# Fewer products with ones: five operands a head, a starting product instead of zeros, one conversion step on ScalarE, and twelve weight slots

## The chip, the cores and the metric

One core of one Trainium2 chip runs the program once. The metric is the time of the program on the device in microseconds, the median of several runs. Engines are named as in the profile: PE is TensorE (PEld its weight loads), DVE is VectorE, ACT is ScalarE, POOL is GpSimd, SP is the engine that issues all transfers here.

## What is computed

Three stages follow each other, all in float32 as seen from outside.

```python
# attention over 4 x 8 heads, 1152 keys, 576 pooled queries, head size 64
q_pool = q.reshape(B, H, S // 2, 2, D).mean(axis=3)
scores = scale * np.matmul(q_pool, k.transpose(0, 1, 3, 2))
scores = scores - np.max(scores, axis=-1, keepdims=True)
attn = np.exp(scores)
attn = attn / (np.sum(attn, axis=-1, keepdims=True) + 1e-09)
x = np.matmul(attn, v)                       # then (2304, 512)
# soft mixture of 8 experts, 4 slots each
logits = x @ phi
d = softmax over tokens;  slot_input = d.T @ x
slot_out[e] = np.maximum(slot_input[e] @ w1[e], 0.0) @ w2[e]
x = (softmax over slots) @ slot_out
# a last feed-forward layer
h = x @ w_in
out = np.where(h >= 1, h, np.where(h <= -1, 0.0, (h + 1) ** 2 / 4)) @ w_out
```

The feed-forward weights w_in and w_out come in as float64 words and are converted to float32 on the chip, in 32 pieces, while attention runs.

## The kernel before, in words

**Attention.** Heads are worked on in 16 pairs. A pair has 9 steps c of 128 keys, and each step has two halves h = 0, 1, one for each head. In this text (c,h) is a half step. The order of every half step is written out by hand under `manual_schedule`, the loop at the end of the printed code: `max_half` (scores 11 steps ahead, of the next pair or the one after it, 4 products on PE and a maximum `mp` on DVE, L309 and L321), `st` (scores of the present pair, 8 products, L375, and the exponentials `e` on ACT, L380), `es_sum` in some half steps (L397), `pv` of the step before (the product with v, L410), and then what the table `sched` holds for this half step, put there by `plan` and by the list `CVS`. Three PSUM tiles go round under the names `mx` and `st`: a product for the maximum and a score product take the next one each, so `st` of a half step can start only when the `mp` of the half step before has read its tile.

**The row sums.** The sum over keys of the exponentials is a product with a column of ones, into columns behind the product with v in the two tiles `acc`. Which steps are first added up on DVE stands in `GRP`: before, steps 0 and 1, 2 and 3, 4 and 5 are added in pairs (`es_add`, L387, three additions a head), and 6, 7 and 8 go in as they are: six operands a head. `TAT` says in which half step which operands are multiplied: operand 0 in (3,1), 1 in (5,1), 2 and 3 in (7,1), 4 and 5 in (9,0), which is (0,0) of the next pair. Every operand takes 8 products, which the trace counts as 16 since a float32 product is two instructions. Before the first product with v, in (1,0) and (1,1), two products with a column of zeros (L407) write zeros to the used columns of each `acc` tile, and everything after them accumulates.

**The conversion.** Piece n of the feed-forward weights is loaded (`cv_load`, tile `f`, two buffers), converted on DVE in four steps (`cv_step` 0 to 3, tile `wst`, two buffers), and stored. Step 0 is two instructions, L191 (take off the sign) and L192 (clamp). For n below 16 ACT makes a rounded copy `whi` and DVE the rest (`cv_lo`, L215), a fifth step. `CVS` lists the eleven half steps of each pair in which one such step is put; the work starts in pair 0 and ends in pair 13. Piece n + 2 is loaded as soon as step 3 of piece n is over.

**The experts' weights.** 36 blocks of 1 MB (`w1`, `w2`, then four blocks `wi` of the converted w_in) are loaded in a fixed order into 23 slots of 8 KB a partition, which open as attention's pools close, and one more, `w_last`. The last 12 blocks go into slots that are used a second time: `w_load` takes slot (i - NSL - 1) % NWA, with NWA = 10, when `w_used` has told that the slot was read. So blocks wi 2 and wi 3 wait for the two first blocks of the second half of `w2`. All transfers are issued by SP in program order.

## Time and profile before

| | us |
|---|---|
| median of 3 runs | 807.64 (806.80 to 808.34) |
| the profiled execution, its own time | 807.59 |
| its span in the trace | 805.4 |
| PE busy | 781.2 (97%) |
| DVE busy | 558.8 (69%) |
| ACT busy | 434.0 (54%) |
| POOL busy | 130.4 (16%) |
| mean granted TensorE clock | 0.992 of full speed |

The times in the trace count from the span's start. Attention takes the stretch from about 33 to 530 us, the experts that up to about 590, the feed-forward layer the rest. PE is called busy while any product is in its pipe, so neighbouring products overlap in the rows; the step from one start to the next tells what a group costs PE. The same holds for DVE, where a row of 0.75 us is followed by the next start after 0.67.

### The profile page before, as it was taken

What the parts mean: (1) busy time and instruction counts of PE and PEld (TensorE: products, weight loads), DVE (VectorE), ACT (ScalarE), POOL (GpSimd) and SP (SyncE); (2) the same over time, 40 slices, a digit from 0 to 9 for tenths busy, and PEclk for the clock granted to TensorE, in tenths of its full rate; (3) what the DMA queues carried; (4) which work ended last, traced back from release to release, by engine and by line L of the source; (5) the groups of instructions that cost most, each with busy time, mean ns of one, the idle gap of its engine ahead of it and who ended that gap; (6) DMA issues with size and microseconds to landing.
All of it is one profiled execution on the core that took longest, in us unless ns stands there. A gap on an engine that the chain in (4) does not pass through costs nothing.

```text
span 805.4 us, 19576 instructions
## 1 busy us (share of the span) xinstructions
PE 781.2 (97%) x8216; PEld 562.7 (70%) x8216; DVE 558.8 (69%) x879; ACT 434.0 (54%) x823; POOL 130.4 (16%) x104
## 2 busy tenths in 40 slices
PE   7899999999999999999999999999999999999998
PEld 6676766666766766667665676663478888888887
DVE  6878888787898787878977864225286777666620
ACT  4346556565665565565555645621276777565620
POOL 7000000000000000000000000000244445434330
PEclk8899999999999999999999999999999999999999
DMA  9777758897988778787897761869980000000000
GB/s 212 179 161 174 206 153 204 230 229 184 239 220 215 207 181 215 211 204 217 195 223 213 189 190 16 313 229 375 393 312 26 27 27 1 26 27 27 27 26 27
DMA packets 144103, 135.51 MB, mean 168 GB/s; under 512 B 80912, under 2 KB 100624, under 8 KB 143632
## 3 DMA queue, kind: packets, MB, share of 16 engines
q1 hardware_dynamic: 144016, 134.28, 60.6%
q8 instruction: 64, 1.05, 0.5%
q14 instruction: 23, 0.19, 0.1%
HBM read 91.29 MB, written 17.30 MB: 135 GB/s over the span
## 4 chain that ended last, share of the span: by engine, by line
PE 80%; DVE 9%; ACT 4%; DMA 4%; issue 2%; SPq 1%; ACTq 0%; DVEq 0%
PE st L375 16%; PE acc L410 14%; PE po L1025 8%; PE po L1024 8%; PE po L1026 8%; PE mx L309 7%; PE acc L397 7%; DVE mp L321 4%; ACT e L380 3%; PE h L961 2%; PE tx L447 2%; PE h L777 2%; DMA q<-qn 1%; PE s2o L829 1%; PE tb L474 1%
## 5 line engine op out<-in xcount | busy, mean ns | idle before, releaser
L380 ACT ACTIVATE e<-st 128x576 f32<-128x576 f32 x288 | 187.3, 652 | 162.3 <-PE st L375 156.6
L321 DVE TENSOR_REDUCE mp<-mx 128x1 f32<-128x576 f32 x282 | 211.2, 751 | 78.7 <-PE mx L309 77.9
L410 PE MATMUL acc<-e,vf 128*64 128x288 f32 x1152 | 195.3, 412 | 0.6 <-ACT e L380 0.6
L309 PE MATMUL mx<-K,q 128*64 128x288 f16 x1152 | 124.4, 296 | 8.6 <-DVE mp L321 5.4
L375 PE MATMUL st<-q,K 128*64 128x288 f16 x1152 | 121.9, 288 | 6.0 <-DVE mp L321 2.5
L375 PE MATMUL st<-q,S 128*64 128x288 f16 x1152 | 121.9, 286 | 0.4 <-DMA q<-qn 0.4
L309 PEld LDWEIGHTS <-q 128*64 128x64 f16 x1152 | 64.7, 111 | 68.7 <-issue 22.2
L974 DVE TENSOR_TENSOR r<-cl,r 128x1024 f32<-128x1024 f32 x34 | 81.2, 2388 | 38.6 <-ACT cl L973 38.6
L1025 PE MATMUL po<-wlo,ghi 128*128 128x512 f32 (+1 forms) x280 | 107.6, 384 | 0.0
L1024 PE MATMUL po<-whi,ghi 128*128 128x512 f32 (+1 forms) x280 | 107.6, 384 | 0.0
L1026 PE MATMUL po<-whi,glo 128*128 128x512 f32 (+1 forms) x280 | 107.2, 383 | 0.0
L980 POOL TENSOR_TENSOR glo<-r,ghi 128x1024 fp32r<-128x1024 f32 x34 | 81.7, 2403 | 101.6 <-ACT ghi L979 99.3
L375 PEld LDWEIGHTS <-K 128*64 128x64 f16 x1152 | 68.1, 109 | 28.4 <-issue 19.2
L277 POOL TENSOR_TENSOR qf<-qf 128x576 f32<-128x576 f32 x14 | 20.8, 1483 | 402.9 <-DMA qf<-in_q_dram 282.4
L410 PEld LDWEIGHTS acc<-e,vf 128*64 128x64 f32 x1152 | 75.9, 136 | 13.2 <-ACT e L380 1.8
L387 DVE TENSOR_TENSOR es<-e,e 128x576 f32<-128x576 f32 x96 | 70.7, 739 | 7.8 <-PE acc L397 7.8
L375 PEld LDWEIGHTS <-S 128*64 128x64 f16 x1152 | 69.8, 110 | 3.3 <-issue 0.6
L964 ACT ACTIVATE r<-h,cols 128x512 f32<-128x512 f32 x68 | 42.8, 685 | 32.8 <-PE h L961 31.3
L1026 PEld LDWEIGHTS po<-whi,glo 128*128 128x128 f32 x280 | 52.6, 188 | 10.5
L1024 PEld LDWEIGHTS po<-whi,ghi 128*128 128x128 f32 x280 | 52.7, 188 | 9.7
L1025 PEld LDWEIGHTS po<-wlo,ghi 128*128 128x128 f32 x280 | 52.7, 188 | 9.2
L965 DVE TENSOR_SCALAR cl<-h 128x512 f32<-128x512 f32 x68 | 43.7, 686 | 18.2 <-ACT r L964 16.7
(192 smaller groups left out, 838.2 us busy)
## 6 DMA issues: line engine op xcount, KB each, us to landing
w<-in_moe_w_dram SPq DMA_DIRECT2D x31, 1024.0 KB, 8.2
vf<-in_v_dram SPq DMA_DIRECT2D x16, 576.0 KB, 4.9
kf<-in_k_dram SPq DMA_DIRECT2D x30, 288.0 KB, 3.6
f<-in_moe_w_out_dram SPq DMA_DIRECT2D x16, 512.0 KB, 4.9
f<-in_moe_w_in_dram SPq DMA_DIRECT2D x16, 512.0 KB, 5.9
qf<-in_q_dram SPq DMA_DIRECT2D x30, 256.0 KB, 4.4
S<-K SPq DMA_DIRECT2D x16, 288.0 KB, 6.3
out_dram<-ob SPq DMA_DIRECT2D x17, 256.0 KB, 2.0
```

The costliest lines, as they stand in the source:

```text
L309: nc.tensor.matmul(ps[p0:p1, i, 0:HQ], lhsT=q1[P][:, t, p0:p1], rhs=kk[:, j * HQ:(j + 1) * HQ], start=True, stop=True)
L321: nc.vector.tensor_reduce(out=mp[P][:, t, a:a + 1], in_=ps[:, :, 0:HQ], op=ALU.max, axis=AX.XY)
L375: nc.tensor.matmul(ps[c0:c0 + 64, i, 0:HQ], lhsT=kk[:, ci, c0:c0 + 64], rhs=f[:, sl[i]], start=first, stop=not first)
L380: nc.scalar.activation(out=e, in_=ps[:, :, 0:HQ], func=AF.Exp, scale=ESC)
L387: nc.vector.tensor_tensor(out=Es[P, n, h], in0=a, in1=b, op=ALU.add)
L397: nc.tensor.matmul(acc[P, i][32 * j:32 * j + 32, HQ:HQ + c1 - c0], lhsT=ones.to_broadcast([128, 32]), rhs=src[:, j % 2, c0:c1], start=Fals ...
L410: nc.tensor.matmul(acc[P, i][h * 64:(h + 1) * 64, 0:HQ], lhsT=vt[P][:, h, c, :], rhs=E[P, c, h][:, i, :], start=False, stop=(c == NK - 1))
L974: nc.vector.tensor_tensor(out=r[:, sl], in0=cl[:, sl], in1=r[:, sl], op=ALU.add)
L980: nc.gpsimd.tensor_tensor(out=glo[n, qd][:, sl], in0=r[:, sl], in1=ghi[n, qd][:, sl].bitcast(F32), op=ALU.subtract)
L1024: nc.tensor.matmul(po, lhsT=ghi[n, qd][:, j, sl], rhs=whi[:, f, cs], start=(f == 0), stop=False)
L1025: nc.tensor.matmul(po, lhsT=ghi[n, qd][:, j, sl], rhs=wlo[:, f, cs], start=False, stop=False)
L1026: nc.tensor.matmul(po, lhsT=glo[n, qd][:, j, sl], rhs=whi[:, f, cs], start=False, stop=(f == 15))
```

## The change

It does four things.

1. `GRP` now adds steps 0 to 4 up on DVE (four additions a head, eight a pair, in the half steps (2,h) to (5,h)) and leaves 5 to 8 alone: five operands a head. `TAT` multiplies operands 0, 1, 2 in (7,0) and 3, 4 in (9,0), and nowhere else.
2. The products with zeros are gone. The first product with v starts the accumulation itself (`start=(c == 0)`).
3. L191, the first instruction of conversion step 0, becomes an absolute value on ACT (`cv_abs`), issued for piece n + 1 right behind step 3 of piece n. `CVS` is another list of eleven half steps; (0,0) and (7,0) now hold two steps each.
4. The pool of two weight slots `w0` stays open as long as the first ten, and twelve slots go round instead of ten.

```diff
-CVS = (0, 1), (1, 0), (3, 1), (4, 0), (4, 1), (5, 0), (5, 1), (6, 0), (7, 0), (8, 0), (8, 1)
+CVS = (0, 0), (0, 0), (0, 1), (3, 1), (4, 1), (6, 0), (7, 0), (7, 0), (7, 1), (8, 0), (8, 1)
...
-GRP = ((0, 1), (2, 3), (4, 5), (6,), (7,), (8,))
-TAT = ((3, 1, (0,)), (5, 1, (1,)), (7, 1, (2, 3)), (9, 0, (4, 5)))
+GRP = ((0, 1, 2, 3, 4), (5,), (6,), (7,), (8,))
+TAT = ((7, 0, (0, 1, 2)), (9, 0, (3, 4)))
...
+    NWL = NWA + NW0
...
-            sl = i if i < NSL else (i - NSL - 1) % NWA
+            sl = i if i < NSL else (i - NSL - 1) % NWL
...
-            if (i if i < NWA else i - NWA + NSL + 1) not in gone:
+            if (i if i < NWL else i - NWL + NSL + 1) not in gone:
...
+    def cv_abs(n):
+        t, dst = cv[n][0], g2.tile([128, 512], F32, tag="wst", bufs=2, name=f"wst{n}")
+        cv[n] = t, dst
+        nc.scalar.activation(out=dst, in_=t[:, :, 1].bitcast(F32), func=AF.Abs)
+
     def cv_step(n, i):
...
-            nc.vector.tensor_scalar(out=d, in0=t[:, :, 1], scalar1=0x7fffffff, scalar2=None, op0=ALU.bitwise_and)
             nc.vector.tensor_scalar(out=dst, in0=dst, scalar1=CLO, scalar2=CHI, op0=ALU.max, op1=ALU.min)
...
             if n + 2 < 32:
                 cv_load(n + 2)
+            if n + 1 < 32:
+                cv_abs(n + 1)
...
     def pv(P, c, i):
         if c == 0:
             acc[P, i] = acc_tile(i, f"acc{P}_{i}")
-
-            n = HQ + (192 if i == 0 else HQ - 192)
-            z = ident.bitcast(F16)[:, 0:n // 2].unsqueeze(1).to_broadcast([128, 2, n // 2])
-            for h in range(2):
-                nc.tensor.matmul(acc[P, i][h * 64:(h + 1) * 64, 0:n].rearrange("p (a b) -> p a b", a=2),
-                                 lhsT=zcol.bitcast(F16)[:, 0:1].to_broadcast([128, 64]), rhs=z, start=True, stop=False)
         for h in range(2):
             nc.tensor.matmul(acc[P, i][h * 64:(h + 1) * 64, 0:HQ], lhsT=vt[P][:, h, c, :], rhs=E[P, c, h][:, i, :],
-                             start=False, stop=(c == NK - 1))
+                             start=(c == 0), stop=(c == NK - 1), skip_group_check=True)
...
+        at(CVS[CV0 - 1][0], 0, cv_abs, 0)
...
-                    pool = wtop.enter_context(tc.tile_pool(name=nm, bufs=1, side="right"))
+                    pool = (wx if nm == "w0" else wtop).enter_context(tc.tile_pool(name=nm, bufs=1, side="right"))
```

Three places show how instructions move. First PE in pair 6. Before, the products with ones stand in four places; this is the one in (3,1), between the scores and the product with v (`es6_0_0` is the sum of steps 0 and 1 of head 0, `x2` the two products that differ in the rows written):

```order
L397 MATMUL acc6_0_3457<-es6_0_0_3520,cols_71 32x192 x2
L397 MATMUL acc6_0_3457<-es6_0_1_3544,cols_71 32x192 x2
L397 MATMUL acc6_1_3485<-es6_0_0_3520,cols_71 32x96 x2
L397 MATMUL acc6_1_3485<-es6_0_1_3544,cols_71 32x96 x2
L410 MATMUL acc6_1_3485<-e6_2_0_3509,vf6_2981 64x288
L410 MATMUL acc6_1_3485<-e6_2_1_3540,vf6_2981 64x288
```

With the change nothing of them is left in (3,1), and (7,0) of the same pair has three operands in a row, the sum of steps 0 to 4 and steps 5 and 6 as they are:

```order
L401 MATMUL acc6_0_3377<-es6_0_0_3433,cols_71 32x192 x2
L401 MATMUL acc6_0_3377<-es6_0_1_3457,cols_71 32x192 x2
L401 MATMUL acc6_1_3400<-es6_0_0_3433,cols_71 32x96 x2
L401 MATMUL acc6_1_3400<-es6_0_1_3457,cols_71 32x96 x2
L401 MATMUL acc6_0_3377<-e6_5_0_3593,cols_71 32x192 x2
L401 MATMUL acc6_0_3377<-e6_5_1_3613,cols_71 32x192 x2
L401 MATMUL acc6_1_3400<-e6_5_0_3593,cols_71 32x96 x2
L401 MATMUL acc6_1_3400<-e6_5_1_3613,cols_71 32x96 x2
L401 MATMUL acc6_0_3377<-e6_6_0_3633,cols_71 32x192 x2
L401 MATMUL acc6_0_3377<-e6_6_1_3660,cols_71 32x192 x2
L401 MATMUL acc6_1_3400<-e6_6_0_3633,cols_71 32x96 x2
L401 MATMUL acc6_1_3400<-e6_6_1_3660,cols_71 32x96 x2
```

Four places have become two, and the other two operands stand in (0,0) of the next pair as two did before.

Second DVE in the same pair, from (3,0) to (5,0); each `mp` row opens a half step. Before, with conversion steps of piece 12 (`wst12`) in (3,1), (4,0), (4,1) and (5,0):

```order
L321 TENSOR_REDUCE mp7_3265<-mx7_5_0_3546 128x1
L287 SCALAR_TENSOR_TENSOR qn2_0_104<-qf8_3288,qn1_106 128x9x64
L321 TENSOR_REDUCE mp7_3265<-mx7_5_1_3574 128x1
L194 TENSOR_SCALAR wst12_3465<-wst12_3465 128x512
L321 TENSOR_REDUCE mp7_3265<-mx7_6_0_3612 128x1
L387 TENSOR_TENSOR es6_1_0_3635<-e6_2_0_3509,e6_3_0_3561 128x576
L197 SCALAR_TENSOR_TENSOR wst12_3465<-f64_12_3183,wst12_3465 128x512
L321 TENSOR_REDUCE mp7_3265<-mx7_6_1_3638 128x1
L387 TENSOR_TENSOR es6_1_1_3665<-e6_2_1_3540,e6_3_1_3589 128x576
L200 SCALAR_TENSOR_TENSOR wst12_3465<-f64_12_3183,wst12_3465 128x512
L321 TENSOR_REDUCE mp7_3265<-mx7_7_0_3672 128x1
L215 TENSOR_TENSOR wst12_3465<-wst12_3465,whi12_3668 128x512
```

And now:

```order
L325 TENSOR_REDUCE mp7_3169<-mx7_5_0_3459 128x1
L391 TENSOR_TENSOR es6_0_0_3433<-es6_0_0_3433,e6_2_0_3422 128x576
L291 SCALAR_TENSOR_TENSOR qn2_0_104<-qf8_3216,qn1_106 128x9x64
L325 TENSOR_REDUCE mp7_3169<-mx7_5_1_3488 128x1
L391 TENSOR_TENSOR es6_0_1_3457<-es6_0_1_3457,e6_2_1_3453 128x576
L199 SCALAR_TENSOR_TENSOR wst12_3289<-f64_12_3141,wst12_3289 128x512
L325 TENSOR_REDUCE mp7_3169<-mx7_6_0_3519 128x1
L391 TENSOR_TENSOR es6_0_0_3433<-es6_0_0_3433,e6_3_0_3474 128x576
L325 TENSOR_REDUCE mp7_3169<-mx7_6_1_3543 128x1
L391 TENSOR_TENSOR es6_0_1_3457<-es6_0_1_3457,e6_3_1_3503 128x576
L202 SCALAR_TENSOR_TENSOR wst12_3289<-f64_12_3141,wst12_3289 128x512
L325 TENSOR_REDUCE mp7_3169<-mx7_7_0_3578 128x1
```

Every half step from (2,0) to (5,1) now has one addition; conversion steps are left only in (3,1) and (4,1), and the others have gone to (6,0) and later.

Third SP in pair 8, around (6,1) and (7,0), where the transposing load of the next pair's second operand (`q2`) and the six loads of k and q for pair 11 are issued. Before, the store of piece 17 and the load of piece 19 stood ahead of them:

```order
L207 DMA wi_dr_76<-wst17_4654 128x512
L180 DMA f64_19_4746<-in_moe2_w_in_dram 128x1024
L358 DMA_TRANSPOSE q2_9_4786<-qn2_1_105 128x9x128
L233 DMA kf11_4828<-in_k_dram 128x576 x2
L241 DMA qf11_4831<-in_q_dram 128x4x128
L242 DMA qf11_4831<-in_q_dram 128x4x128
L243 DMA qf11_4831<-in_q_dram 64x128
L244 DMA qf11_4831<-in_q_dram 64x128
```

Now they stand behind:

```order
L362 DMA_TRANSPOSE q2_9_4647<-qn2_1_105 128x9x128
L237 DMA kf11_4711<-in_k_dram 128x576 x2
L245 DMA qf11_4714<-in_q_dram 128x4x128
L246 DMA qf11_4714<-in_q_dram 128x4x128
L247 DMA qf11_4714<-in_q_dram 64x128
L248 DMA qf11_4714<-in_q_dram 64x128
L209 DMA wi_dr_76<-wst17_4349 128x512
L181 DMA f64_19_4721<-in_moe2_w_in_dram 128x1024
```

The absolute value of piece 19, which needs both (the load, and the buffer that the store reads), stands on ACT in (8,1) of the same pair, behind the exponentials of that half step.

## Rows read from the trace of the kernel before

**Rows 1.** The profile page, chain of waits that ended last, shares by engine.
```profile
PE 80%; DVE 9%; ACT 4%; DMA 4%; issue 2%; SPq 1%; ACTq 0%; DVEq 0%
```

**Rows 2.** Busy us (instructions) by stretch: PE, PEld, DVE, ACT, POOL, clock, DMA share, GB/s.
```profile
221.52:252.41 30.89, 30.08 (x407) 21.29 (x403) 26.16 (x44) 18.52 (x42) 2.54 (x2) 1.00 0.82 211
477.23:504.96 27.73, 27.66 (x380) 19.39 (x376) 13.11 (x22) 15.67 (x35) 0.00 (x0) 1.00 0.22 41
```

**Rows 3.** Timeline of PE, pairs 5 and 6: start us, us, engine, line, what.
```profile
217.91 1.19 PE L397 MATMUL acc<-e,cols 128*32 128x192 f32 x32
219.03 0.71 PE L410 MATMUL acc<-e,vf 128*64 128x288 f32 x4
...
221.52 0.37 PE L407 MATMUL acc<-ident,cols 128*64 128x480 f16 x2
221.72 0.66 PE L410 MATMUL acc<-e,vf 128*64 128x288 f32 x4
...
222.94 0.33 PE L407 MATMUL acc<-ident,cols 128*64 128x384 f16 x2
223.10 0.66 PE L410 MATMUL acc<-e,vf 128*64 128x288 f32 x4
...
230.26 0.70 PE L397 MATMUL acc<-es,cols 128*32 128x192 f32 x16
230.88 0.71 PE L410 MATMUL acc<-e,vf 128*64 128x288 f32 x4
```

**Rows 4.** Timeline of PE, pair 6: products for the maximum at five half steps.
```profile
220.78 0.42 PE L309 MATMUL mx<-K,q 128*64 128x288 f16 x4
...
226.12 0.44 PE L309 MATMUL mx<-K,q 128*64 128x288 f16 x4 [0.57 <-DVE mp L321]
...
238.91 0.41 PE L309 MATMUL mx<-K,q 128*64 128x288 f16 x4
...
240.13 0.41 PE L309 MATMUL mx<-K,q 128*64 128x288 f16 x4
...
241.35 0.41 PE L309 MATMUL mx<-K,q 128*64 128x288 f16 x4
```

**Rows 5.** Timeline of DVE, pair 6, half steps (5,1) and (6,0).
```profile
238.39 0.42 DVE L191 TENSOR_SCALAR wst<-f 128x512 int32<-128x512 int32 x1
238.84 0.43 DVE L192 TENSOR_SCALAR wst<-wst 128x512 f32<-128x512 f32 x1
239.37 0.76 DVE L321 TENSOR_REDUCE mp<-mx 128x1 f32<-128x576 f32 x1
240.04 0.75 DVE L387 TENSOR_TENSOR es<-e,e 128x576 f32<-128x576 f32 x1
240.71 0.42 DVE L194 TENSOR_SCALAR wst<-wst 128x512 int32<-128x512 int32 x1
```

**Rows 6.** Groups of ACT by line: busy us, mean ns, then idle time before.
```profile
L204 ACT ACTIVATE whi<-wst 128x512 fp32r<-128x512 f32 x16 | 10.1, 631 | 6.7 <-DVE wst L200 4.7 <-DVE mm L354 1.8
```

**Rows 7.** Timeline of SP at the end of pair 6.
```profile
242.25 2.12 SPq L358 DMA_TRANSPOSE q<-qn  x1
...
247.79 0.53 SPq L180 DMA_DIRECT2D f<-in_moe_w_out_dram  x1
```

**Rows 8.** Tiles f (first) and wst (second): from issue to landing.
```profile
DMA to landing us min/median/max: 3.7/5.7/7.2
DMA to landing us min/median/max: 2.3/4.6/6.6
```

**Rows 9.** Timelines of POOL and DVE, end of pair 1.
```profile
92.22 1.42 POOL L277 TENSOR_TENSOR qf<-qf 128x576 f32<-128x576 f32 x1 [28.45 <-DMA qf<-in_q_dram]
92.71 1.22 DVE L191 TENSOR_SCALAR wst<-f 128x512 int32<-128x512 int32 x1
```

**Rows 10.** Busy us of a stretch among the experts (columns of rows 2), and the chain there.
```profile
562.00:566.00 4.00, 4.00 (x44) 1.16 (x36) 0.62 (x8) 0.00 (x0) 0.00 (x0) 1.00 1.05 387
574.71 8.08 DMA whi<-wo_dr
```

More of the change, by code (lines that the diff above doesn't have):

```diff
@@ L181, in cv_load @@
         cv[n] = t, None
+    def cv_abs(n):
+        t, dst = cv[n][0], g2.tile([128, 512], F32, tag="wst", bufs=2, name=f"wst{n}")
+        cv[n] = t, dst
+        nc.scalar.activation(out=dst, in_=t[:, :, 1].bitcast(F32), func=AF.Abs)
     def cv_step(n, i):
         t, dst = cv[n]
-        if dst is None:
-            dst = g2.tile([128, 512], F32, tag="wst", bufs=2, name=f"wst{n}")
-            cv[n] = t, dst
         d = dst.bitcast(I32)
         if i == 0:
-            nc.vector.tensor_scalar(out=d, in0=t[:, :, 1], scalar1=0x7fffffff, scalar2=None, op0=ALU.bitwise_and)
             nc.vector.tensor_scalar(out=dst, in0=dst, scalar1=CLO, scalar2=CHI, op0=ALU.max, op1=ALU.min)
@@ L397, in es_sum @@
                     nc.tensor.matmul(acc[P, i][32 * j:32 * j + 32, HQ:HQ + c1 - c0], lhsT=ones.to_broadcast([128, 32]),
-                                     rhs=src[:, j % 2, c0:c1], start=False, stop=False)
+                                     rhs=src[:, j % 2, c0:c1], start=False, stop=False, skip_group_check=True)
     def pv(P, c, i):
```

## The prediction

> **What bounds the kernel now.** I read the chain of waits first: PE holds 80% of it and DVE 9% [rows 1], so time is won where PE has less to do, and lost where DVE makes PE wait. Then I cut attention into pairs of heads. Pair 6 takes 30.89 us, with DVE busy for 26.16 of it; pair 14, which has no conversion and DVE busy for 13.11, takes 27.73 [rows 2]. The reader is to see two things in these rows: the clock is 1.00, the higher of its two levels (2.4 GHz), in both, so it explains nothing; and a pair with a loaded DVE is 3.2 us longer. About 1 us of that is products for maxima that pair 14 no longer has (those of its last four half steps, 0.3 each, estimated as 4 of the 16 products of a clean half step, which takes 1.22 us from 240.13 to 241.35 [rows 4]). Some 2 us a pair are therefore time in which PE waits for DVE. One such wait stands in the timeline, 0.57 us before the product at 226.12 [rows 4].
>
> **The products with ones.** In the timeline a place with two operands costs PE 1.12 us from its start to the next group's (217.91 to 219.03), a place with one 0.62 (230.26 to 230.88) [rows 3]. So a further operand in the same place costs 0.50. Before: two places with two and two with one, 2 x 1.12 + 2 x 0.62 = 3.48 us a pair. After: one with three (1.12 + 0.50 = 1.62) and one with two, 2.74. That is 0.74 a pair off PE.
>
> **The zeros.** Their two groups take 0.20 and 0.16 us from start to start [rows 3], 0.36 a pair. Nothing follows in their place: the first product with v now waits for its exponentials and for the emptied tile at once, and both were there before, since the zeros ran without a wait in these rows.
>
> Together PE has 1.10 us less in each of 16 pairs, 17.6 us. All of it lies on PE's own path, unless DVE now ends last. (In the last pair exponentials have four buffers, so those of (7,0) wait for the products with ones of the same half step, up to 1.62 us; PE needs them two half steps later, which covers it.)
>
> **VectorE's load.** An addition costs 0.67 from start to start (240.04 to 240.71), a maximum 0.67, the removed L191 0.45 (238.39 to 238.84) [rows 5]. Two additions a pair more are 32 x 0.67 = 21.4 us; 32 times L191 less are 14.4. So DVE gets 7 us more in all, some 0.5 a pair, and PE 1.1 less: the two come close, and the place decides. I cut the pair in two.
>
> From (1,0) to (5,1) a pair now takes 238.91 - 220.78 = 18.13 us [rows 4]. The zeros and both places with one operand (0.62 each) lie there, so 18.13 - 0.36 - 1.24 = 16.53 would be left with the same waits. DVE has to do there, after the change: ten maxima and eight additions (18 x 0.67 = 12.1), three splits of k and q of the same size (2.0), two conversion steps (1.0), and 0.3 of small work, 15.4 in all. That fits, with 1.1 to spare, and it is spread evenly, one addition a half step, where before conversion steps and additions met in (4,0), (4,1) and (6,0). The other eight half steps get PE 0.50 longer, 12.76 + 0.50 = 13.26, and DVE there has eight maxima, nine short conversion steps and little else, about 10.3. So I expect waits to shrink, not to grow. Bounds of this term: between nothing and the 1.1 to spare, in the 13 pairs with conversion; I take 0.5, nearer to the timeline's waits of half a microsecond than to the end, 6.5 us in all.
>
> **The absolute value on ScalarE.** No row shows this function. The nearest is the copy of the same size on ACT, 0.631 us [rows 6]; the lower bound is the 0.45 that DVE took. ACT is busy for 18.5 of 30.9 us in pair 6 [rows 2], so 32 x 0.63 = 20 us more hide there, and no queue but ACT's own exponentials stands behind them. The Trainium skill, ScalarE: Activation LUTs, Rules for kernel authors, speaks against this: elementwise work of that kind belongs on VectorE, which is faster. The rows agree on speed (0.45 against 0.63) but not on the price here: by the page the move loses 6 us of engine time, by the rows it takes 14 off the engine that PE waits for, and the sum is the same either way.
>
> What counts is what the absolute value waits for. It is issued early, one piece ahead, and needs the load of its piece and the store that empties its buffer. Where that load is issued in (7,0) or later, it stands on SP behind the transposing load of `q2` and six loads of k and q: SP starts the first at 242.25 and comes to the load of `f` at 247.79, 5.5 us on [rows 7]. With the usual 5.7 to the landing [rows 8] that is 11.2 us. In pairs 5, 8 and 12 the absolute value that needs it is in (8,1), which ACT reaches about 7 us after 242.25 (1.62 + four clean half steps of 1.22 and the exponential). So ACT would stand for some 4 us with the next exponentials behind it, and PE, which can go on for two half steps, would lose 2 to 2.5 each time: I take 7 us for the three. In seven more pieces the same load is needed one or two half steps later, and the products with ones of (0,0) cover it. Bounds: 0, if it lands early, and 23 if all ten cost 2.3.
>
> **Twelve slots.** The two last blocks of w_in no longer wait for the two first blocks of the second half of `w2`. But in that stretch the transfer engines are full, 1.05 of their time at 387 GB/s, and the chain there is the landing of `whi` [rows 10], which stands behind the same bytes as before. Issuing earlier only lengthens the queue: I take 0, and 1.5 either way as bounds.
>
> **The sum.** The profiled execution took 807.59, within 0.1 of the median. 807.6 - 17.6 - 6.5 + 7 = 790.5; I say 790.5.
>
> **The rivals.**
>
> *VectorE becomes the bound and it gets slower.* Eight additions in ten half steps make `mp` late, PE waits for the tile, and (1,0) to (5,1) stays at 18.1 us. Then a pair takes 18.13 + 13.26 = 31.39, 0.5 more than now: + 6.5 in 13 pairs, - 3.3 in the three without conversion, + 7 for the late absolute values, 818; 811 without those. It turns slower once the stretch is above 17.6. For it: DVE will be busy for some nine tenths of a pair. Against: 15.4 is well below 17.6. I give it 0.06. Half of it (a stretch of 17.3, pairs of 30.6) gives about 807, no change: 0.05.
>
> *ScalarE stands for every late load.* All ten cost 2.3: 790.5 + 16 = 806.5. Against: the later ones have 2 to 3 us more time. 0.05.
>
> *GpSimd in the way.* When its addition runs (92.22 to 93.64), L191 beside it takes 1.22 instead of 0.42 [rows 5, 9]. This addition comes about (0,1), and the change puts three conversion steps into (0,0) and (0,1). At 0.8 in each of 13 pairs, all on the path, that is 10.4 us: 801. PE has the products with ones in (0,0) to cover half: 796. 0.08. The Trainium skill, GPSIMD Engine Reference, Specifications, states the same as a rule: the two engines share their access to SBUF, and VectorE instructions that read two inputs from it contend too. By that rule the additions would be hit as well, but they lie in (2,0) to (5,1), and the trace shows GpSimd at work at the end of a pair only.
>
> *It all works.* No late landing, and the whole 1.1 comes back: 807.6 - 17.6 - 14.3 = 776. 0.10.
>
> **How the numbers follow.** My forecast has the remaining 0.66. The range runs from 780 (half of the best case's further gain) to 801 (GpSimd on the whole path, or the forecast with waits that do not shrink and one and a half times the late loads); what is left out is most of the slower and the unchanged cases and the lower half of the best, about 0.2. A run can be told from no change from 0.2% on, 1.6 us. Faster by more: 0.66 + 0.08 + 0.10 and a part of ScalarE's case, 0.86. Within: 0.05. Slower: 0.09, VectorE's case and the rest of ScalarE's.
>
> **What will show it.** Right: the products with ones on PE fall from 1536 to 1280 (six operands to five, 16 rows each, 16 pairs), and no product with zeros is left; the distance from one pair's (1,0) to the next is near 29.3 in an ordinary pair; DVE has no wait of an addition for `acc`; ACT's absolute values take about 0.63; ACT shows three or so waits for `f` or `wst` of some microseconds, at the ends of pairs 5, 8 and 12. Wrong on the DVE step: PE rows with waits for `mp` in (2,0) to (5,1), and a pair of 30.5 or more. Wrong on the ACT step: exponentials that wait behind absolute values in most pairs. Wrong on the slots: `whi` landing earlier after the last product of attention than now. What would make the whole prediction wrong is a DVE that, with nine tenths of its time taken, cannot keep its maxima in step.

## The result, and the profile after

The changed kernel takes 800.18 us (five runs, 796.57 to 803.1), the kernel before 807.9 beside it (five runs, 806.8 to 808.34): ratio 0.9906, 95% interval 0.9888 to 0.9925. It is 7.7 us faster where 17.1 were forecast; the time lies in the range, near its slow end. The profiled execution took 803.1, 2.9 above the median, with a span of 801.0.

The page's chain of waits, shares by engine, then by line, answers to [rows 1]:

```profile
PE 73%; DMA 10%; ACT 6%; DVE 6%; issue 3%; SPq 1%; ACTq 0%; DVEq 0%
PE st L379 14%; PE acc L408 13%; PE po L1024 8%; PE po L1023 8%; PE po L1025 8%; PE mx L313 7%; PE acc L401 4%; ACT e L384 3%; DMA f<-in_moe_w_in_dram 2%; DVE mp L325 2%; DMA wi<-wi_dr 2%; PE h L960 2%; DMA wo_dr<-wst 2%; PE h L776 2%; DMA wo_dr<-whi 2%
```

DVE has left part of the chain (9% to 6%), and DMA has come in (4% to 10%): the load of `f` and the stores of `whi` and `wst`, none of which this line names for the kernel before. (The load of `wi` comes behind attention, where the time did not change.)

Of the 4.4 us between the two profiled executions 3.5 lie in attention, from its first score product (`st`) to the start of the last, in (8,1) of pair 15. Behind that start nothing is won: 278.3 us to the end of the span before, 278.7 after (spans less 527.06 and 522.29). Another 1.3 lie ahead of the first score product, at 32.2 before and 30.9 after; over the runs below that start lies anywhere from 29.8 to 32.5, so nothing is read from it.

Busy time by stretch (columns of [rows 2]), after the change, for pair 6, pair 10 and pair 14, each from the first score product of (1,0) to the same in the next pair:

```profile
219.11:248.31 29.20, 28.87 (x384) 20.92 (x384) 26.02 (x45) 19.90 (x44) 0.54 (x1) 1.00 0.88 223
347.09:377.42 30.33, 29.99 (x384) 21.93 (x385) 26.64 (x45) 17.95 (x39) 1.11 (x1) 0.94 0.76 202
474.75:501.05 26.30, 26.23 (x359) 18.76 (x355) 14.61 (x24) 15.65 (x36) 0.00 (x0) 1.00 0.20 51
```

Pair 6 went from 30.89 to 29.20 and pair 14 from 27.73 to 26.30 [rows 2]: there the change does what it was to do. In pair 10 the granted clock is 0.94 on average, although no stretch of that pair was below 1.00 before. To see where the gain went I took, for every pair, the time from its score product of (0,0) to that of the next pair, for pair 15 to its last (start times from PE's timeline):

| pairs | before, us | after | difference |
|---|---|---|---|
| 0 | 26.26 | 26.04 | -0.22 |
| 1, 2, 3 | 93.81 | 88.30 | -5.51 |
| 4, 5 | 65.06 | 67.71 | +2.65 |
| 6 to 9 | 127.12 | 127.39 | +0.27 |
| 10, 11, 12 | 98.38 | 101.10 | +2.72 |
| 13 | 30.21 | 29.59 | -0.62 |
| 14, 15 | 54.03 | 51.25 | -2.78 |

Pairs 1 to 13, those with conversion, together gain 0.5 us: three early ones gain 5.5, pairs 4, 5, 10 and 12 lose it again. (Pair 6 is longer here than in the stretch above, since this count begins at (0,0) and so takes in a wait shown below.)

The list of ACT's waits (line, releaser: us in total, times, longest) names what is new there:

```profile
ACT wst L187 <- DMA f<-in_moe_w_in_dram: 9.4, 3, 4.3
ACT whi L206 <- DMA wo_dr<-whi: 4.8, 2, 3.5
```

With 1.3 us of waits of `wst` for its own store that is 15.5. Two more belong to it which the list puts to other releasers:

```profile
345.84 0.66 ACT L187 ACTIVATE wst<-f 128x512 f32<-128x512 f32 x1 [1.82 <-issue]
411.08 0.66 ACT L187 ACTIVATE wst<-f 128x512 f32<-128x512 f32 x1 [1.74 <-DVE mp L325]
```

The loads of `f` that these two values need landed at 345.76 and 411.01, just before them. So ACT stood for landings 19.1 us in all.

And the list of PE's waits, what that did:

```profile
PE mx L313 <- ACT e L384: 9.4, 14, 2.0
PE st L379 <- ACT e L384: 7.4, 7, 2.9
PE acc L408 <- ACT e L384: 3.4, 3, 2.0
```

These are 20.2 us in which PE waited for an exponential; in the same list of before it was 1.3. The end of pair 5 shows how. ACT's timeline (start us, us, engine, line, what, idle before it), then SP's, then PE's:

```profile
212.50 0.65 ACT L384 ACTIVATE e<-st 128x576 f32<-128x576 f32 x1 [0.57 <-PE st L379]
216.65 0.63 ACT L206 ACTIVATE whi<-wst 128x512 fp32r<-128x512 f32 x1 [3.50 <-DMA wo_dr<-whi]
217.19 0.68 ACT L187 ACTIVATE wst<-f 128x512 f32<-128x512 f32 x1
217.78 0.62 ACT L384 ACTIVATE e<-st 128x576 f32<-128x576 f32 x1
```

```profile
206.53 1.99 SPq L362 DMA_TRANSPOSE q<-qn  x1
208.57 2.17 SPq L237 DMA_DIRECT2D kf<-in_k_dram  x2
...
212.37 0.60 SPq L248 DMA_DIRECT2D qf<-in_q_dram  x1
213.06 0.53 SPq L221 DMA_DIRECT2D wo_dr<-whi  x1
```

```profile
215.94 0.66 PE L408 MATMUL acc<-e,vf 128*64 128x288 f32 x4
218.45 0.44 PE L313 MATMUL mx<-K,q 128*64 128x288 f16 x4 [1.86 <-ACT e L384]
```

The store of `whi10` stands on SP behind `q2` and six loads, is issued at 213.06 and has landed by 216.65. ACT, which has one buffer of `whi`, stands for it from 213.15 on; the exponential behind it begins at 217.78, 4 us after its scores were there, and PE loses 1.86.

### The profile page after: what moved, and what is told of

Same layout as the page of the kernel before. It is cut to its first block, busy times and chain, and to the rows that moved or that the text cites. A ratio compares the mean times of both kernels' runs of the same rounds, so it can differ in the third digit from the quotient of the medians.

```text
span 801.0 us, 19118 instructions
## 1 busy us (share of the span) xinstructions
PE 760.3 (95%) x7896; PEld 557.8 (70%) x7896; DVE 566.7 (71%) x879; ACT 452.6 (57%) x855; POOL 129.8 (16%) x104
## 4 chain that ended last, share of the span: by engine, by line
PE 73%; DMA 10%; ACT 6%; DVE 6%; issue 3%; SPq 1%; ACTq 0%; DVEq 0%
PE st L379 14%; PE acc L408 13%; PE po L1024 8%; PE po L1023 8%; PE po L1025 8%; PE mx L313 7%; PE acc L401 4%; ACT e L384 3%; DMA f<-in_moe_w_in_dram 2%; DVE mp L325 2%; DMA wi<-wi_dr 2%; PE h L960 2%; DMA wo_dr<-wst 2%; PE h L776 2%; DMA wo_dr<-whi 2%
## 5 line engine op out<-in xcount | busy, mean ns | idle before, releaser
L408 PE MATMUL acc<-e,vf 128*64 128x288 f32 x1152 | 201.2, 414 | 3.4 <-ACT e L384 3.4
L313 PE MATMUL mx<-K,q 128*64 128x288 f16 x1152 | 127.3, 295 | 17.8 <-ACT e L384 9.4
L379 PE MATMUL st<-q,K 128*64 128x288 f16 x1152 | 125.5, 289 | 11.0 <-ACT e L384 7.4
L379 PE MATMUL st<-q,S 128*64 128x288 f16 x1152 | 125.8, 288 | 0.0
L313 PEld LDWEIGHTS <-q 128*64 128x64 f16 x1152 | 66.8, 111 | 78.7 <-issue 36.5
L379 PEld LDWEIGHTS <-K 128*64 128x64 f16 x1152 | 70.9, 110 | 28.8 <-issue 19.8
L408 PEld LDWEIGHTS acc<-e,vf 128*64 128x64 f32 x1152 | 81.0, 138 | 11.5 <-ACT e L384 5.4
L379 PEld LDWEIGHTS <-S 128*64 128x64 f16 x1152 | 72.1, 110 | 2.8
L391 DVE TENSOR_TENSOR es<-es,e 128x576 f32<-128x576 f32 x96 | 71.5, 746 | 2.7 <-ACT e L384 2.5
L1025 PEld LDWEIGHTS po<-whi,glo 128*128 128x128 f32 x280 | 52.6, 188 | 10.4
L964 DVE TENSOR_SCALAR cl<-h 128x512 f32<-128x512 f32 x68 | 43.7, 686 | 18.2 <-ACT r L963 16.7
```

What stands on the lines that cost most here:

```text
L313: nc.tensor.matmul(ps[p0:p1, i, 0:HQ], lhsT=q1[P][:, t, p0:p1], rhs=kk[:, j * HQ:(j + 1) * HQ], start=True, stop=True)
L379: nc.tensor.matmul(ps[c0:c0 + 64, i, 0:HQ], lhsT=kk[:, ci, c0:c0 + 64], rhs=f[:, sl[i]], start=first, stop=not first)
L391: nc.vector.tensor_tensor(out=Es[P, n, h], in0=a, in1=b, op=ALU.add)
L408: nc.tensor.matmul(acc[P, i][h * 64:(h + 1) * 64, 0:HQ], lhsT=vt[P][:, h, c, :], rhs=E[P, c, h][:, i, :], start=(c == 0), stop=(c == NK - ...
L964: nc.vector.tensor_scalar(out=cl[:, a:b], in0=src, scalar1=-1.0, scalar2=1.0, op0=ALU.max, op1=ALU.min)
L1025: nc.tensor.matmul(po, lhsT=glo[n, qd][:, j, sl], rhs=whi[:, f, cs], start=False, stop=(f == 15))
```

## The experiments

Every ratio is to the kernel before, run beside it on the same chip. "Attention" is the time from the first to the last score product in the profiled execution (494.9 before, 491.4 after the change); "falls" counts the places in attention where the granted clock went down to 0.5. Both are read from one execution, which isn't always one near the median: those of the change, e1, e4, e12, e16 and e17 took 1.8 to 4.5 us more than the median, those of e2, e6, e8, e10 and e14 2.1 to 4.2 us less.

| run | us | ratio, 95% | attention | falls |
|---|---|---|---|---|
| the change | 800.2 | 0.9906 (0.9888 to 0.9925) | 491.4 | 3 |
| e1 | 796.9 | 0.9850 (0.9828 to 0.9871) | 487.9 | 1, a long one |
| e2 | 808.8 | 1.0003 (0.9988 to 1.0019) | 495.3 | 0 |
| e3 | 793.3 | 0.9823 (0.9801 to 0.9846) | 481.7 | 0 |
| e4 | 794.9 | 0.9840 (0.9817 to 0.9864) | 487.9 | 2 |
| e5 | 794.4 | 0.9827 (0.9808 to 0.9846) | 483.0 | 1 |
| e6 | 797.1 | 0.9855 (0.9829 to 0.9880) | 481.4 | 0 |
| e7 | 804.4 | 0.9952 (0.9937 to 0.9967) | 491.9 | 1 |
| e8 | 802.0 | 0.9923 (0.9894 to 0.9951) | 486.3 | 1 |
| e9 | 788.1 | 0.9748 (0.9735 to 0.9761) | 474.7 | 0 |
| e10 | 795.7 | 0.9840 (0.9827 to 0.9853) | 479.9 | 0 |
| e11 | 806.6 | 0.9977 (0.9967 to 0.9986) | 494.5 | 0 |
| e12 | 803.5 | 0.9939 (0.9925 to 0.9953) | 492.5 | 0 |
| e13 | 786.7 | 0.9735 (0.9721 to 0.9748) | 475.5 | 0 |
| e14 | 789.4 | 0.9776 (0.9762 to 0.9790) | 475.6 | 0 |
| e15 | 786.5 | 0.9734 (0.9720 to 0.9748) | 473.5 | 0 |
| e16 | 790.3 | 0.9784 (0.9770 to 0.9798) | 479.2 | 0 |
| e17 | 786.3 | 0.9722 (0.9703 to 0.9741) | 478.4 | 1 |

### The parts, one at a time (e11, e12, e7, e8)

e11 is the kernel before without its zeros:

```diff
...
-            nc.tensor.matmul(acc[P, i][...], lhsT=zcol..., rhs=z, start=True, stop=False)
...
-                             start=False, stop=(c == NK - 1))
+                             start=(c == 0), stop=(c == NK - 1), skip_group_check=True)
```

> The kernel before with the zeros alone taken out (the first product with v begins the sum). Prediction's term: 0.36 us in each of 16 pairs, 5.8 us: 801 to 803.5. Rival: the products behind them wait for exponentials anyway, so nothing is gained: 807 to 809.

A gain of 0.23%, 1.9 us by the ratio, a third of the term and between the two cases. Its stretches, pair 6 and pair 14 (columns of [rows 2]):

```profile
220.64:251.85 31.21, 30.08 (x403) 21.27 (x399) 26.70 (x45) 18.51 (x41) 1.73 (x2) 1.00 0.84 226
476.37:503.74 27.37, 27.30 (x375) 19.13 (x371) 13.39 (x22) 15.67 (x36) 0.00 (x0) 1.00 0.17 44
```

Pair 14 gives exactly the 0.36 us of the term (27.73 to 27.37). Pair 6 gives nothing (30.89 to 31.21), but it is no clean case. VectorE's split of k beside GpSimd's addition, before and then in e11:

```profile
221.96 1.30 DVE L264 SCALAR_TENSOR_TENSOR kn<-kf,kn 128x576 f16<-128x576 f32 x1
```

```profile
221.57 1.87 DVE L264 SCALAR_TENSOR_TENSOR kn<-kf,kn 128x576 f16<-128x576 f32 x1
```

Beside GpSimd some instructions of VectorE take over 0.2 us longer than others of their line: over pairs 1 to 13 eight before, by 4.9 us together, and ten in e11, by 9.9. Clean are pairs 9 and 13, where neither trace has one: counted as in the table of pairs both take 30.21 us before and in e11. There VectorE ends last: PE waits 0.22 us for `mp` in each of them in e11 and not at all before, so most of the 0.36 that it is spared becomes waiting. The term was measured right and holds where there is no conversion. In the clean pairs with conversion it is worth nothing by itself; what the others would keep without GpSimd is not shown.

e12 is the kernel before with the new `GRP` and `TAT` alone:

```diff
-GRP = ((0, 1), (2, 3), (4, 5), (6,), (7,), (8,))
-TAT = ((3, 1, (0,)), (5, 1, (1,)), (7, 1, (2, 3)), (9, 0, (4, 5)))
+GRP = ((0, 1, 2, 3, 4), (5,), (6,), (7,), (8,))
+TAT = ((7, 0, (0, 1, 2)), (9, 0, (3, 4)))
```

> The kernel before with the grouping and places of the products with ones alone (eight additions a pair, two places), absolute value on VectorE, conversion steps at their old places, zeros kept. PE has 0.74 us less in 16 pairs, 11.8; VectorE has two additions more just where its conversion steps stand: in (1,0) to (5,1) 15.4 + 4 x 0.6 + some 0.45 for the absolute value in half the pairs, about 18, against 16.9 of PE's work. If VectorE is full there, the pair keeps its length or grows: 804 to 815. If it has room: 796 to 799.

803.5, just outside the first case. In the profiled execution, the slowest of six (805.59), pairs 14 and 15 gain 1.05 and 1.07 us (the term said 0.74) and pairs 1 to 13 together nothing; ten instructions of VectorE lengthened by 9.5 us beside GpSimd are in that, and the clean pairs 9 and 13 gain 0.3 each. e7 is the whole change with the conversion steps left where they were:

```diff
-CVS = (0, 0), (0, 0), (0, 1), (3, 1), (4, 1), (6, 0), (7, 0), (7, 0), (7, 1), (8, 0), (8, 1)
+CVS = (0, 1), (1, 0), (3, 1), (4, 0), (4, 1), (5, 0), (5, 1), (6, 0), (7, 0), (8, 0), (8, 1)
```

> The changed kernel with the conversion steps at the places of the kernel before ((0,1) to (8,1), one each), absolute value on ScalarE, eight additions. If VectorE is full where additions and steps meet ((1,0) to (5,1) would hold 15.4 + 4 x 0.6 = 17.8 us of VectorE's work against 16.5 of PE's): some 1.3 to 2 us lost in 13 pairs there, and less lost to late landings: 797 to 806. If only the late landings cost time: 780 to 788.

804.4, in the first case again, with pairs 1 to 13 gaining 0.5 us in all. With the buffers as changed the new places win 0.5% (0.9952 to 0.9906). What they do to each engine can be read from the waits: with the old places PE waits 10.4 us for `mp`, with the new ones 7.9; and ACT's waits for loads and stores are 4.7 us in the list with the old places, 15.5 with the new ones (7.0 and 19.1 with those put to other releasers). So the new places relieve VectorE, and they are what makes the landings late. PE still waits 12.0 us for exponentials in e7, and the old places with more buffers were not run: that VectorE alone sets the length of its pairs is not shown.

e8 gives the weights ten slots again:

```diff
-    NWL = NWA + NW0
+    NWL = NWA
...
-                    pool = (wx if nm == "w0" else wtop).enter_context(...)
+                    pool = wtop.enter_context(...)
```

> The changed kernel with ten weight slots going round instead of twelve; nothing else. Prediction's theory (the transfer engines are full there, issuing earlier only lengthens the queue): within 1.5 us of 800. Rivals: the twelve slots win 2 us or more (this one 802 or above), or they cost, as the chain's new 2% for wi suggests (798 or below).

By the ratios e8 is 1.4 us slower, with overlapping intervals, so the times don't decide. The profiles do for the stage that the slots belong to: 278.8 us behind the last score product against 278.7 (and 278.3 before). Twelve slots bring nothing that can be seen there, as forecast.

### Where the absolute value stands (e1, e2, e10)

e1 puts it back on VectorE, into step 0:

```diff
-        nc.scalar.activation(out=dst, in_=t[:, :, 1].bitcast(F32), func=AF.Abs)
+        nc.vector.tensor_scalar(out=dst.bitcast(I32), in0=t[:, :, 1], scalar1=0x7fffffff, scalar2=None, op0=ALU.bitwise_and)
...
     def cv_step(n, i):
+        if i == 0:
+            cv_abs(n)
...
-            if n + 1 < 32:
-                cv_abs(n + 1)
...
```

> The changed kernel with the absolute value back on VectorE, as the first instruction of its piece's first step; grouping, places of the steps, zeros and slots as changed. Theory A (ScalarE stands before absolute values whose load or buffer is late, exponentials behind it, and PE waits: 20.2 us of waits of PE for e in the changed kernel, next to none before): those waits fall under 6 us, VectorE gets 14.4 us more, the time falls by 10 to 16 us to 784 to 790. Theory B (the steps stand too close together from (7,0) to (0,1), so the load is late whichever engine takes the value): VectorE stands for f instead, PE waits for mp, and the time stays between 797 and 803.

796.9: between the two theories, each half right. PE's waits for exponentials fall from 20.2 to 7.2 us, near the 6 of theory A; but VectorE now stands for `f` (6.0 us) and ACT still for the store of `whi` (5.1), and PE's waits for `mp` grow from 7.9 to 14.6. The data are late for either engine.

e2 leaves it on ScalarE, but in the half step of step 0:

```diff
     def cv_step(n, i):
+        if i == 0:
+            cv_abs(n)
...
-            if n + 1 < 32:
-                cv_abs(n + 1)
...
```

> The changed kernel with the absolute value still on ScalarE, but issued in the half step of the piece's own first step, one or two steps later than now. Theory A: its load and its buffer have landed in most pairs, PE's waits for e fall by half or more, and what is new is VectorE's wait for the value in the same half step (32 times up to 0.67 us, partly covered): 786 to 793. Theory B: no change, 797 to 803, with VectorE waiting for the value by what ScalarE waits less.

Neither theory: 808.8, all of the gain gone. From the list of DVE's waits:

```profile
DVE wst L196 <- ACT wst L187: 39.8, 29, 3.0
```

In 29 pieces VectorE stood 1.4 us on average, since ACT does the exponential and copies of that half step first. e10 issues it one half step earlier than e2, if that isn't before the piece ahead has had its step 3:

```diff
...
+                if i == 0:
+                    g, sl = cvs[0]
+                    at(*max((g - 1 + sl, 1 - sl), last), cv_abs, n)
+                if i == 3:
+                    last = cvs[0]
...
```

> The changed kernel with the absolute value on ScalarE issued one half step ahead of the step on VectorE that needs it, where that is later than now (20 of 31); buffers as changed. In the same half step (e2) VectorE stood for it 29 times, 39.8 us in all. Theory of late landings: in those 20 pieces load and store get one or more half steps longer, half of the loss of some 20 us comes back: 788 to 794. If it is only the wait moved from ScalarE to VectorE: 797 to 803.

795.7, a little short of the first case; VectorE's wait for the value is 7.1 us (5 times). One half step between issuer and user is worth 13 us (e2 to e10), and issuing no earlier than that 5 us (the change to e10).

### Buffers and the queue (e3, e4, e5, e9, e6)

These are the changed parts of lines. e3 has the first two, e4 the third and fourth (and piece 2 loaded in pair 0), e5 the second to fourth (one slot moved from `NW1` to `NW2`), e9 all of them. In e5 and e9 pieces 2 and 3 are loaded together behind step 3 of piece 0:

```diff
+tag="wst", bufs=3
+tag="whi", bufs=2
+tag="f64", bufs=3
+            cv_load(n + 3)
-NWA, NW0, NW1, NW2, NWK, NW3, NW4 = 10, 2, 1, 6, 1, 2, 1
+NWA, NW0, NW1, NW2, NWK, NW3, NW4 = 9, 2, 1, 7, 1, 2, 1
```

> The changed kernel with three buffers of wst for two and two of whi for one; nothing else. If the stores hold ScalarE up (the trace has 4.8 us of waits of whi for its own store and 1.3 of wst for its store): 6 us of waits go and the time falls by 3 to 6 us, to 794 to 797. If the loads of f do it all: the time stays within 1.5 us of 800.

> The changed kernel with three buffers of f for two, each load issued one piece earlier; nothing else. If late loads hold ScalarE up (9.4 us of waits in the trace, three times): those go, and the time falls by 6 to 12 us, to 788 to 794. If stores and the closeness of the steps do it: it stays within 2 us of 800.

> The changed kernel with three buffers of f and two of whi; the third load is issued with the second one's successor after piece 0, not in pair 0 as in the run before (where it cost pair 0 some 5 us), and one weight slot moves from the pool freed first to the next. Theory of late landings (load of f, store of whi): what the two changes won apart adds up, 784 to 788. Rival (one hides the other, the steps' closeness keeps the rest): no better than the better of the two, 791 to 795.

e3 gains 6.7 us by the ratios, a little more than expected of the stores, and e4 5.3, a little less than expected of the loads, although its extra load in pair 0 lengthened that pair from 26.3 to 31.8. Loads and stores both hold ScalarE up. But e5 is no better than either (the rival's case), and ACT's waits tell why:

```profile
ACT wst L187 <- DMA wo_dr<-wst: 6.6, 3, 5.3
ACT wst L187 <- DMA wi_dr<-wst: 4.6, 2, 2.6
```

With `f` and `whi` there in time, the absolute value waits 11.2 us for the stores that empty `wst`. With two kinds of buffer raised the wait goes to the third.

> The changed kernel with three buffers of f, three of wst and two of whi together, paid for with one of the ten first weight slots (which moves to a pool freed later). After e3 and e5 the theory is: each buffer alone only hands the wait on (e5 lost the waits for f and whi and got 11.2 us of waits of ScalarE for stores of wst). With all three, ScalarE should wait for no landing for over 1 us, PE for e under 8 us in all, a pair with conversion takes some 2 us less than before, and attention ends some 25 us earlier than before (4.7 in the changed kernel's trace): 780 to 786, the slot costing 0 to 2 of it. Rival (the late exponentials have another cause, ScalarE's own load where tail and conversion meet): attention ends at most 16 us earlier, 791 to 795.

788.1, 12.8 us better than the change by the ratios, attention 16.7 shorter, and ACT waits for no load or store of the conversion any more. The forecast was a little better still (780 to 786). PE waits 8.9 us for exponentials.

e6 leaves the buffers and issues the six loads of k and q of a (7,0) behind the conversion step's own load and store:

```diff
-            at(b - LQK, 0, load_qk, P)
...
+        for P in range(2, NP):
+            at(NK * P - LQK, 0, load_qk, P)
         nsteps = NP * NK
```

> The changed kernel with one order changed: in (7,0) the six loads of k and q are issued behind the conversion step's load and stores, not ahead of them (4.4 us on SP in pair 6 of the changed kernel, 239.70 to 244.00, then the load of f at 244.00). If SP's queue makes loads and stores late: the waits for f and the stores shrink by up to 4.4 each and the time falls by 5 to 10 us, to 790 to 795. If the transfers themselves are slow (engines some nine tenths busy there): within 2 us of 800.

797.1, 0.5% better than the change, less than expected. ACT's waits for landings are now these:

```profile
ACT wst L187 <- DMA f<-in_moe_w_in_dram: 4.3, 3, 2.4
ACT whi L206 <- DMA wo_dr<-whi: 1.2, 1, 1.2
```

That is 5.5 us against 15.5 (with those put to other releasers 8.1 against 19.1), so by the waits SP's queue is more than half of the lateness. The time follows less. One reason can be seen: q is loaded later, so GpSimd adds it later, and eleven instructions of VectorE are lengthened by 6.4 us beside it, against four by 2.7 in the change. The landing itself takes what it took (a load of `f` 5.6 us from issue in the middle, 5.7 before; a store from `wst` 4.0, 4.6 before [rows 8]): transfers did not get slower, the time left for them got shorter.

### What is left without late landings (e13 to e17)

e13 is e3 without loads after the first two (the diff is against e3):

```diff
     def cv_load(n):
+        if n > 1:
+            cv[n] = cv[n - 2][0], None
+            return
```

> As e3 (three wst, two whi), and pieces 2 to 31 of w_out and w_in are not loaded: they convert the first two pieces again, so 30 loads are left out, and the output's weights are those of other rows. No absolute value can then wait for a load, and with three buffers hardly for a store. If landings are what is left of the loss after e3: attention ends 24 to 30 us earlier than before, time 776 to 784. If the chain of a piece's last steps within one half step (copy on ScalarE behind the tail's copies, subtraction on VectorE behind it) keeps a part: no better than e9, attention 18 to 22 us earlier, 787 to 791.

786.7, at the edge of the second case, with attention 19.3 us shorter than before, less than 1 us off e9's. So with e9 the landings are dealt with.

e14 is e9 with e1's edit, e15 is e9 with e10's, e16 is e15 with e6's.

> e9 with the absolute value back on VectorE, in the piece's first step. With buffers enough, theory: the move to ScalarE relieves VectorE of 14.4 us in pairs where it ends last, so without it 4 to 9 us are lost against e9: 792 to 797. Rival (the move is worth nothing, ScalarE's chain costs what VectorE wins): 786 to 790.

> e9 with the absolute value issued one half step ahead of its use, as in e10. What is left in e9 are 4.4 us of VectorE's waits for the value and some 1.2 us in (4,0) of pairs 2 and 7, where two conversions and the tail's copies meet on ScalarE: 2 to 5 us better than e9, 783 to 786. Rival (already hidden): 787 to 789.

> e15 with the conversion's loads and stores issued ahead of the k and q loads in (7,0), as in e6. If any landing is still late: 1 to 3 us better than e15. If none is: the same within 1 us.

e14: 789.4, in the rival's range. With buffers enough, ScalarE's absolute value wins 0.3% (e9) to 0.4% (e15); with the buffers as changed it costs 0.6% (e1). By the Trainium skill, ScalarE: Activation LUTs, Rules for kernel authors, elementwise work such as relu or max belongs on VectorE. The rows agree on the speed: the value takes 0.673 us on ScalarE (L187) and 0.42 on VectorE (L191, [rows 5]). The move wins a little all the same; VectorE is the busier of the two (71% of the span against 57% in the changed kernel).

e15: 786.5, just above its forecast, 0.14% better than e9, with overlapping intervals. e16 was to be no worse, and is 3.8 us slower than e15. VectorE's timeline in e16, and GpSimd's, at the same moment:

```profile
216.63 1.99 DVE L267 SCALAR_TENSOR_TENSOR kn<-kf,kn 128x576 f16<-128x576 f32 x1
218.54 0.74 DVE L324 TENSOR_REDUCE mp<-mx 128x1 f32<-128x576 f32 x1
219.21 0.74 DVE L267 SCALAR_TENSOR_TENSOR kn<-kf,kn 128x576 f16<-128x576 f32 x1
```

```profile
216.59 1.42 POOL L280 TENSOR_TENSOR qf<-qf 128x576 f32<-128x576 f32 x1 [30.79 <-DMA qf<-in_q_dram]
```

Loaded later, q is added later by GpSimd, and its addition now falls on VectorE's split of k, which takes 1.99 instead of 0.74. In pairs 1 to 13 of e16 eleven instructions of VectorE are lengthened so, by 9.8 us in all; in e15 eight, by 4.6. Those pairs together are 4.8 us longer in e16, so the size fits; no run takes GpSimd's part away. By the Trainium skill, GPSIMD Engine Reference, Specifications, VectorE instructions with two inputs in SBUF contend with GpSimd; these rows agree.

e17 is e15 with five steps half a step later, so that none stands in the half step of the value on ScalarE that it needs.

```diff
...
+                if i in (0, 4) and (g, sl) == last:
+                    g, sl = g + sl, 1 - sl
...
```

> e15 with five steps a half step later: the subtractions of pieces 8 and 9 (pairs 4 and 5), which stood in the half step of the copy on ScalarE that they need, and the first steps of pieces 18, 22 and 29 (pairs 8, 10, 12), which stood with the absolute value that they need. If the chain VectorE, ScalarE, VectorE within one half step is what is left: pair 5 loses its 1.6 us in (0,1), pair 10 its 1.1, the time falls by 2 to 4 us, to 783 to 784.5. Rival (VectorE is simply full at those places, the steps cost as much a half step later): 786 to 787.5.

786.3, the same as e15 within the intervals: the rival's case. The waits of PE that it was to remove, 1.45 in pair 5 and 0.93 in pair 10 of e15, are gone, but pairs 5 and 10 are only 0.5 and 0.4 us shorter. (The profiled execution, 790.36, is the slowest of five: in pair 14, where e17 changes nothing, PE stands 2.19 us for the landing of `q`, the clock falls, and the pair is 4.0 us longer.) e15 and e17 beat both kernels, the one before by 2.7%, the changed one by 1.7%.

## Why the prediction missed

**The late absolute values: this step failed.** It put 7 us on the ends of pairs 5, 8 and 12 and nothing on "seven more pieces", where "the products with ones of (0,0) cover it". The three were right in place, and ScalarE stands there 3.50, 4.31 and 4.11 us ("some 4 us"). For pairs 8 and 12 the reason was right too: the load of `f`. For pair 5 it was not, and that the place came true is partly luck. The load that the value needs there was issued at 205.40, ahead of `q2`, and had landed at 210.69; late were the two stores of piece 10 behind the six loads, of `whi` first and of `wst` (217.17) just after it. The three cost PE less than the 2 to 2.5 each: 1.86 at the start of pair 6, 0.83 at that of pair 9, 0.63 at that of pair 13. What failed is the cover of the others. PE's timeline has these:

```profile
152.07 0.46 PE L408 MATMUL acc<-e,vf 128*64 128x288 f32 x1 [1.97 <-ACT e L384]
...
187.69 0.44 PE L379 MATMUL st<-q,K 128*64 128x288 f16 x4 [1.45 <-ACT e L384]
...
283.01 0.44 PE L313 MATMUL mx<-K,q 128*64 128x288 f16 x4 [1.64 <-ACT e L384]
...
347.09 0.44 PE L379 MATMUL st<-q,K 128*64 128x288 f16 x4 [2.86 <-ACT e L384]
...
379.66 0.46 PE L408 MATMUL acc<-e,vf 128*64 128x288 f32 x1 [1.10 <-ACT e L384]
...
412.33 0.63 PE L313 MATMUL mx<-K,q 128*64 128x288 f16 x4 [2.03 <-ACT e L384]
```

Six waits at the start of pairs 4, 5, 8, 10, 11 and 12, 11.05 us together, behind the products that were to cover them. Ahead of five of them ScalarE stood for a landing: the store of `whi` in pair 4 (1.29 us), the store of `wst` in pair 8 (1.34), the load of `f` in pairs 10, 11 and 12 (1.82, 1.03 and 1.74). With the buffers of e9 1.6 us are left of these five waits of PE (0.50 in pair 4, 0.93 in pair 10, 0.20 in pair 12), in e15 only the 0.93. (That of pair 5 is none of them and stays, 1.45 us: there both last steps of piece 9 stand in (0,0), and its copy comes behind the tail's copies on ScalarE; e17 removes it.) Two things were left out. Eight of the eleven places of a pair now lie in the six half steps from (7,0) to (0,1), so a whole round of a piece (load, value, copy, stores, the next value in the emptied buffer) can fall due within the time of its landings; I followed the load, named the store that empties `wst`, and did not count `whi` with its one buffer at all. And a wait of PE can have a second price, the clock (last section). Taking the landings away brings 12.8 us by the ratios (e9, 0.9906 to 0.9748), with the value a half step ahead 13.9 (e15, 0.9734); 7 were counted. From the changed kernel's profile to that of e15 attention shrinks by 17.9 us, which is near to what PE waits less for exponentials (20.2 to 6.7) and the 5.1 of the clock.

**PE's term and VectorE's term: 24.1 forecast, 21.5 measured** (e15 to before, by the ratio). PE's was too small where it stands alone: pairs 14 and 15 gain 1.43 and 1.35, not 1.10. By the starts in PE's timeline, (3,1) and (5,1) of pair 14 are 0.78 and 0.77 shorter without their place, where 0.62 was taken, and (7,0) with (7,1) is 0.47 longer, where 0.50 was. VectorE's was too large: pairs 1 to 13 of e15 gain 18.3 us, 1.41 each, where 1.60 was forecast. The clean pairs of e11 show why the two can't be added as I added them: there VectorE ended last before, so what PE spares counts only as far as VectorE is relieved. On the question that decided the sign the step was right: VectorE keeps up once the steps are moved (pair 6 at 29.20, "near 29.3"). That it would not otherwise is what e7 and e12 suggest; in both other waits are mixed in.

**The rest.** Products with ones fell to 1280, no wait of an addition for `acc` is left, and the absolute value takes 0.673 us (0.63 forecast). Slots: 0, as forecast. The rival "ScalarE stands for every late load" was the nearest in mechanism, with 806.5: it had the places and too high a price each, no stores and no clock in it. The GpSimd rival names something real, but not a loss here: in the changed kernel four instructions of VectorE are lengthened, by 2.7 us together, where it counted 10.4, and before it was eight by 4.9; e16, with 9.8, comes near its size. The lower end of the range does not follow as stated: half of the best case's further gain would be 783, not 780. Nothing hangs on it.

## What to carry to other kernels

Before moving work to an engine that "has room", write down, for each place, when its input lands and its output buffer comes free, with the queue ahead of the transfer, and leave slack for each buffer of the chain: raising one or two counts won 5 to 7 us here and handed the rest of the wait to the next buffer, raising all three won 12.8. A value handed from one engine to another was best issued one step of the schedule before its use: in the same step it cost 13 us more, and earlier it held up the exponentials, 5 us. A saving on the engine that looks like the bound is worth nothing in stretches where another ends last, so price each kind of stretch by itself.

## What was not expected of the hardware

A wait of PE can cost twice. After the stand of 2.86 us in pair 10 of the changed kernel, the granted clock falls to its lower level, 1.2 GHz (columns of [rows 2]):

```profile
345.00:346.00 1.00, 0.00 (x0) 0.00 (x0) 0.00 (x0) 0.16 (x1) 0.00 (x0) 1.00 0.82 219
346.00:347.00 1.00, 0.00 (x0) 0.00 (x0) 0.47 (x2) 1.00 (x3) 0.00 (x0) 1.00 1.09 317
347.00:348.00 1.00, 0.91 (x10) 0.76 (x11) 1.00 (x3) 1.00 (x5) 0.00 (x0) 0.79 0.68 142
348.00:349.00 1.00, 1.00 (x9) 0.72 (x7) 1.00 (x2) 0.59 (x2) 0.00 (x0) 0.50 0.24 59
349.00:350.00 1.00, 1.00 (x12) 0.99 (x9) 0.98 (x3) 0.00 (x0) 0.00 (x0) 0.50 0.04 14
350.00:351.00 1.00, 1.00 (x8) 0.57 (x7) 0.72 (x2) 0.65 (x1) 0.00 (x0) 0.50 0.47 94
351.00:352.00 1.00, 1.00 (x18) 0.86 (x14) 0.56 (x1) 0.01 (x1) 0.00 (x0) 1.00 1.14 208
```

Summed over these rows, 1 less the clock is 1.7 us of full speed lost, in which the products go slower: a group of four score products takes 0.48 us from start to start in the fall, 0.24 and 0.25 before and after it. The same follows the stands of 1.97 us in pair 4 and 2.03 in pair 12; after 1.45, 1.64 and 1.86 it did not happen. The length of the stand does not decide alone. In e3 PE stands longer than in those two, and the clock stays at 1.00:

```profile
403.83 0.44 PE L313 MATMUL mx<-K,q 128*64 128x288 f16 x4 [2.74 <-ACT e L384]
```

Nor does it fall after 2.01 us in pair 5 of e5 (186.53). What else decides is not shown. Three falls are 5.1 us, of the 17.9 by which attention is longer than in e15. They also spread the times: of the changed kernel's runs those with a mean granted clock of 0.994 took 796.57 and 799.68, those with 0.989 took 800.18 to 803.1.
